# Half-step preparation of a squared-ReLU attention: one pair of v split eight steps earlier, and the first z block's scaling taken out of the opening

## The chip, the cores and the metric

The kernel runs on one core of a Trainium2 chip. The metric is the device time of one execution in microseconds (us). The kernel before took 1279.15 us (median of 3 runs, 1277.88 to 1280.24). Engines are named as the profile names them: PE multiplies matrices, PEld loads its weights, DVE and ACT are the two elementwise engines that matter here, SP issues the DMAs. Each engine works through its own list of instructions in order, and waits where an instruction needs something from another engine.

## The reference

Two stages stand behind each other. The first is an attention without softmax, in which keys and queries are the same array z, and the second is a soft mixture of experts on its output:

```
scores = (1/S) * z @ z.T                # per batch: 8 batches, S = 2496 tokens, 64 wide
attn   = max(scores, 0) ** 2
x      = u * (attn @ v)                 # v, u: 256 wide
logits = x @ phi                        # 32 slots; softmax over tokens and over slots
slot_input = softmax_tokens(logits).T @ x
slot_out   = relu(slot_input @ w1[e]) @ w2[e]      # 8 experts, 4 slots each
out        = softmax_slots(logits) @ slot_out
```

Inputs and outputs are 32-bit floats.

## The kernel before

**Tiles.** A batch's tokens stand in five blocks of 512 (j or p from 0 to 4). A chunk is one block of queries. A "half" is one chunk of queries against 256 keys, that is two key tiles of 128. A chunk has 10 halves, a batch 50 (the last batch 60), and `halves` is the list of all of them, with the number k counting through. The keys of v come in ten pairs of tiles per batch, `v_{batch}_{pair}`; a half uses one pair, or half of what such a pair covers in two neighbouring halves.

**One half** goes through `prepare(k)` (line 430) and `sums_halves` or `sums_whole` (line 541 and below). In `prepare`, PE multiplies z with z into a score tile `sc` (`scores`), ACT applies the ReLU and then the square (`r<-sc`, `r<-r` in the profile), ACT or DVE casts the result to 16 bits (`ph`, the high part), and DVE subtracts that from the 32-bit value (`pl`, the low part). PE then adds three products to `acc`: high v times `ph`, low v times `ph`, high v times `pl`. Because z times z is symmetric, a prepared half is also turned by DVE (`y<-r`), stored, and read back for the chunk that meets it the other way round; such a "turned" half needs no scores, only the cast and the subtraction.

**Order.** The main loop (line 1026) goes through the halves h. At step h it issues transfers, prepares half h+2 (h+3 from step 18 on) and multiplies half h. In `sums_halves` the twelve matmuls of phase 0 come first, then the scores of the half that is being prepared, then the twelve of phase 1. A list `behind` holds work that runs at the end of a `prepare`, and `landing[step]` puts work there. Every instruction of PE, ACT, DVE and SP stays in the order in which the program writes it (`InOrder`).

**v and z in two parts.** Each pair of v is loaded in 32 bits (`vr`), multiplied with a power of two per pair (`v_by`), and split into a high part by ACT (`v<-vr,v_by`) and a low part by DVE (`v<-vr,v_by,v`). The same is done with z. For batches 1 to 7 the table `v_at` (line 895) gives the step of the batch before, at which each of the ten pairs is split; numbers from 50 on lie in the batch itself.

**The opening.** Batch 0 has no batch before it. Its z blocks stay in `zraw`, slices of the tile `cw`. `measure_z` finds a power of two for each block (`z_by`), `raise_z(p)` (line 977) multiplies block p with it in place on DVE (`cw<-cw,z_by`), and the first 12 halves take their scores from these blocks in 32 bits. The first two halves go another way: `first_scores`, a square, and `plain_sums` in 32 bits with unscaled v, while v is still being measured. `scale_v` then finds v's common factor: one small matmul on PE (`idle<-ident,few`) and five small DVE operations. `keep_busy(n)` issues 2n matmuls of ones whose result nobody reads. After half 2 is prepared, the opening multiplies z blocks 2, 3 and 4 in a row, then prepares half 3, and the main loop begins.

All four engines are called through one helper, so nearly all rows of the profile carry line 74; rows are told apart by engine and tile name.

Of the kernel before, what the change touches and what calls it, by code (L numbers as in the profile page):

```python
# [8 lines left out]
F32 = mybir.dt.float32  # L9
# [5 lines left out]
ALU = mybir.AluOpType  # L15
# [3 lines left out]
P = 128  # L19
# [5 lines left out]
KT = 20  # L25
# [6 lines left out]
NP = KT // 4  # L32
# [45 lines left out]
def attn_soft_moe_kernel(ctx, tc, uT, v, zz, phi, ww, outT):  # L78
# [9 lines left out]
    cpool = ctx.enter_context(tc.tile_pool(name="cpool", bufs=1))  # L88
# [14 lines left out]
    zt, vt_, zraw, vraw = {}, {}, {}, {}  # L103

    nudge = cpool.tile([P, 1], F32, name="nudge")
    ones = nc.const_aps.tensor(1.0, [P, 512], BF16)

    def pair(name, n):
# [318 lines left out]
                start=(k == 0 and t == 0), stop=(k == 1 and t == 1),  # L427
            )

    def prepare(k, r=None):  # L430

        x = halves[k]
        n = x.ch[2]

        parts = [slice(0, 2)]
        if x.turned:
            whole = arriving.pop(k)
            run(middle)
        elif r is not None:
            run(middle)  # L440
            act.activation(r, r, AF.Square)
            whole = r.rearrange("p h (a r) -> p h a r", r=P)
        else:
            r = wa.tile([P, 2, QC], F32, tag="r", name=f"r_{k}", bufs=4)
            ps, m = scores(k)
            for h in parts:
                act.activation(r[:, h, :m], ps[:, h, :m], AF.Relu, scale=2.0**-22)
                run(middle)
                act.activation(r[:, h, :m], r[:, h, :m], AF.Square)
            whole = r[:, :, :m].rearrange("p h (a r) -> p h a r", r=P // 2 if x.borrows else P)  # L450
        hi, lo = high_low(k)
        m = QC if x.padded else n
        hc, lc = (t[:, :, :m].rearrange("p h (a r) -> p h a r", r=P) for t in (hi, lo))
        cast = act.copy if x.turned or (x.turns and x.at % 3 and k > 2) else dve.tensor_copy
        run(turning)
        pieces = [(whole, slice(0, P), cast)]
        if x.borrows:
            lent = arriving.pop(k)
            pieces = [(lent, slice(0, P // 2), act.copy), (whole, slice(P // 2, P), dve.tensor_copy)]
        for h in parts:  # L460
            for src, cols, cast in pieces:
                cast(hc[:, h, :, cols], src[:, h])
                dve.tensor_sub(lc[:, h, :, cols], src[:, h], hc[:, h, :, cols])
        pend[k] = hi, lo
        if x.turns:
            key = x.b, x.ch[0], x.p
            first = key not in staged
            if first:
                staged[key] = turns_sb.tile([P, 16, 4, NS], F32, tag="y", name=f"y_{k}")
            y = staged[key]  # L470

            def turn():
                dve.transpose(
                    y.rearrange("p m i q -> p i m q")[:, 2 * x.w : 2 * x.w + 2],
                    r.rearrange("p h (m q) -> p h m q", q=NS),
                )
                if not first:
                    stores.append((k + (k < 2 * NP), lambda: store(key)))

            if k < 2 * NP:  # L480
                turning.append(turn)
            else:
                turn()
        if x.lends:
            y = turns_sb.tile([P, 4, 2, 2, NS], F32, tag="yd", name=f"yd_{k}", bufs=1)
            dve.transpose(
                y.rearrange("p a j i q -> p i a j q"),
                r.rearrange("p h (a i q) -> p h a i q", i=4, q=NS)[:, :, :, 2:4],
            )
            stores.append((k - 1, lambda: lend(x, y)))  # L490
        run(behind)
# [49 lines left out]
    def sums_halves(k, acc, phase, before):  # L541


        x = halves[k]
        todo = [[], []]
        hi, lo = pend[k]
        for t, kt in enumerate(x.tiles):
            vt = vt_[x.b, kt // 2][:, kt % 2]
            hh, lh, hl = (vt[:, 0], hi[:, t]), (vt[:, 1], hi[:, t]), (vt[:, 0], lo[:, t])
            if kt < KT - 1:  # L550
                for h in range(2):
                    todo[h] += [hh, lh, hl]
            else:

                todo[0] += [hh] if phase else [hh, lh]
                todo[1] += [hl] if phase else [lh, hl]
        for i in range(len(todo[0])):
            for h, rows in enumerate(HALF):
                vp, pp = todo[h][i]
                c = h ^ phase ^ side[0]  # L560
                mm = pe.matmul(
                    totals(acc, c, x), vp[rows, c * P : (c + 1) * P], columns(pp[rows], x),
                    start=(x.starts and phase == 0 and i == 0),
                    stop=(x.ends and phase == 1 and i == len(todo[0]) - 1),
                )
                if before is not None:
                    await_(mm, before)
                    before = None
        if phase == 0:
            turn = nc.gpsimd.nop()  # L570
            await_(turn, mm)
            return turn
        side[0] ^= 1
# [317 lines left out]
    for b in range(1, B):  # L891
        base, order = (b - 1) * 2 * NP * NQ, BLOCKS[b == B - 1]
        z_at = [27, 28, 29, 30, 39 if b == B - 1 else 41]
        v_from = [23, 24, 25, 26, 27, 28, 29, 32, 33, 34]
        v_at = [41, 42, 43, 44, 45, 46, 48, 50, 52, 54]
        if b == B - 1:
            v_at = [42, 43, 44, 45, 46, 48, 52, 53, 41, 50]
        for i, (j, at) in enumerate(zip(order, z_at)):
            splits.setdefault(base + 9 + 2 * i, []).append((load_z, b, j, [base + 12 + 2 * i, base + at]))
        for i, (start, at) in enumerate(zip(v_from, v_at)):  # L900
            splits.setdefault(base + start, []).append(
                (load_v, b, i, [base + start + 1, base + at, base + at])
            )
        later[base + 23] = lambda b=b: add_bounds(b, next_acc(), slice(0, NP))
        later[base + 24] = lambda b=b: factors(b, accs[-1], slice(0, NP))
        later[base + 36] = lambda b=b: largest(b)
        later[base + 39] = lambda b=b: scale_v(b, ms_ps.tile([P, 2, 512], F32, tag="ms", name=f"mx_{b}"))
# [57 lines left out]
    def keep_busy(n):  # L965
        for _ in range(n):
            for h, rows in enumerate(HALF):
                pe.matmul(plain[:, h], ones[rows, 0:P], ones[rows], start=True, stop=True)
# [8 lines left out]
    def raise_z(p):  # L977
        dve.tensor_scalar_mul(zraw[0, p], zraw[0, p], z_by[0][:, p : p + 1])
# [9 lines left out]
        factors(0, idle, js)  # L988

    measure_z(slice(0, 1))  # L990
    raise_z(0)
    keep_busy(3)
    acc = next_acc()
    r0, relu = first_scores(0, scale=2.0**-30)
    relu()
    act.activation(r0, r0, AF.Square)
    r1, relu = first_scores(1, acc, scale=2.0**-30)
    relu()
    keep_busy(4)
    measure_z(slice(1, NP))  # L1000
    raise_z(1)
    dve.tensor_mul(r1, r1, r1)
    plain_sums(0, r0, plain, 0)
# [6 lines left out]
    first_v.pop()(dve)  # L1010
    largest(0)
    plain_sums(1, r1, plain, 0)
    scale_v(0, idle)
    plain_sums(1, r1, plain, 1)
    prepare(2, r2)
    split_first_v()
    split_first_v()
    for p in range(2, NP):
        raise_z(p)
    ratio = few[0][:, 3:4]  # L1020
    dve.tensor_scalar_mul(ratio, v_by[0][:, 0:1], 2.0**16)
    xg_[0] = wk.tile([P, 2, 1024], F32, tag="xg", name="xg_0")
# [3 lines left out]
    for h, x in enumerate(halves):  # L1026
        if x.begins and h:
            chunk = h // (2 * NP)
            acc = accs[chunk] if chunk < len(accs) else next_acc()
        last = len(halves) - h  # L1030
        transfers(h)
        if x.b < NW_OWN and h % (2 * NP * NQ) == 2 * NP * (NQ - 1) + 5:
            load_w(x.b)
        if h < 2:
            continue
        weights(last)
        if work and (x.at > 1 or last <= 20):
            work.pop(0)()
        behind.extend(landing.pop(h, ()))
        ahead = [k for k in range(h + 2 + (h > CATCH), h + 3 + (h >= CATCH)) if k < len(halves)]  # L1040
        split_first_v()
        if ahead and not halves[ahead[0]].turned:
            turn = sums_halves(h, acc, 0, None)
            prepare(ahead.pop(0))
            sums_halves(h, acc, 1, turn)
        else:
            if ahead and not x.ends:
                prepare(ahead.pop(0))
            elif not ahead:
                run(middle)  # L1050
                run(behind)
                between_last(3 - last)
            sums_whole(h, acc)
        if x.ends:
            finish_chunk(x.b, x.ch, acc)
        for k in ahead:
            prepare(k)
        if h in FIRST_Z:
            z_splits.pop(FIRST_Z[h])()
        del pend[h]  # L1060
# [303 lines left out]
```

## Time and profile before

| | us |
|---|---|
| median of 3 runs | 1279.15 |
| the profiled execution's own time | 1278.43 |
| its span, first to last instruction | 1276.6 |
| PE busy in the span | 1247.4 (98%) |
| DVE busy | 1099.7 (86%) |
| ACT busy | 930.2 (73%) |
| PE waiting for DVE's `pl`, whole span | 3.3 in 5 waits |
| PE waiting for DVE's `v`, whole span | 2.3 in 7 waits |
| PE waiting for ACT's `ot`, in the last stage | 11.2 in 14 waits |

The busy time of PE counts each matmul's own duration, and two matmuls on the two halves of PE's rows run side by side, so the pace of PE is read from the starts of its rows rather than from its busy share. A row of the timeline gives the start, the duration, the engine, the operation, "out<-in", how many instructions are merged in the row, and in brackets how long the engine sat idle before it and for whom.

### The profile page before, as it was taken

What the parts mean: (1) busy time and instruction counts of PE and PEld (TensorE: products, weight loads), DVE (VectorE), ACT (ScalarE), POOL (GpSimd) and SP (SyncE); (2) the same over time, 40 slices, a digit from 0 to 9 for tenths busy, and PEclk for the clock granted to TensorE, in tenths of its full rate; (3) what the DMA queues carried; (4) which work ended last, traced back from release to release, by engine and by line L of the source; (5) the groups of instructions that cost most, each with busy time, mean ns of one, the idle gap of its engine ahead of it and who ended that gap; (6) DMA issues with size and microseconds to landing.
All of it is one profiled execution on the core that took longest, in us unless ns stands there. A gap on an engine that the chain in (4) does not pass through costs nothing.

```text
span 1276.6 us, 27277 instructions
## 1 busy us (share of the span) xinstructions
PE 1247.4 (98%) x10931; PEld 634.7 (50%) x10931; DVE 1099.7 (86%) x1594; ACT 930.2 (73%) x1209; POOL 3.7 (0%) x22
## 2 busy tenths in 40 slices
PE   9999999999999999999999999999999999999984
PEld 4445454545445444555445454454545445445752
DVE  7888899789998899889998899898998899886663
ACT  6878797687958788586977778587885879664553
POOL 0000000000000000000000000000000000000000
PEclk9999999999999999999999999999999999999985
DMA  5769668794879757795779757987488766889769
GB/s 167 222 185 300 219 151 252 223 295 129 219 256 299 226 154 203 244 315 189 185 219 293 238 170 180 288 281 262 122 238 246 287 184 159 262 245 337 276 260 383
DMA packets 132942, 298.83 MB, mean 234 GB/s; under 512 B 14416, under 2 KB 35408, under 8 KB 120784
## 3 DMA queue, kind: packets, MB, share of 16 engines
q1 hardware_dynamic: 132816, 297.10, 75.1%
q8 instruction: 85, 1.39, 0.4%
q14 instruction: 41, 0.34, 0.1%
HBM read 162.04 MB, written 113.77 MB: 216 GB/s over the span
## 4 chain that ended last, share of the span: by engine, by line
PE 88%; DVE 6%; ACT 2%; issue 2%; DMA 1%; DVEq 0%; ACTq 0%; SPq 0%
PE acc L74 71%; PE sc L74 10%; PE lg L74 2%; DVE y L74 2%; PE pf L74 2%; DVE pl L74 2%; ACT r L74 1%; PE plain L74 1%; DVE v L74 1%; ACT ot L74 1%; PE po L74 1%; PE h L74 1%; DVE ph L74 1%; DMA outT<-ot 0%; ACT ph L74 0%
## 5 line engine op out<-in xcount | busy, mean ns | idle before, releaser
L74 PE MATMUL acc<-ph,v 64*128 64x512 f16 (+4 forms) x5004 | 935.9, 368 | 2.4 <-DVE v L74 2.3
L74 PEld LDWEIGHTS <-v 64*128 64x128 f16 (+1 forms) x7506 | 490.6, 95 | 500.4 <-issue 39.6
L74 PE MATMUL acc<-pl,v 64*128 64x512 f16 (+5 forms) x2502 | 621.8, 368 | 3.4 <-DVE pl L74 3.3
L74 DVE TENSOR_TENSOR pl<-r,ph 128x1024 f16<-128x1024 f32 (+1 forms) x408 | 464.9, 1146 | 103.8 <-ACT ph L74 79.9
L74 ACT CAST ph<-r 128x1024 f16<-128x1024 f32 (+1 forms) x285 | 288.4, 1019 | 129.0 <-DMA r<-turned 69.5
L74 ACT ACTIVATE r<-sc 128x1024 f32<-128x1024 f32 (+1 forms) x241 | 228.1, 947 | 115.5 <-PE sc L74 109.8
L74 ACT ACTIVATE r<-r 128x1024 f32<-128x1024 f32 (+1 forms) x241 | 237.8, 987 | 6.8
L74 DVE STREAM_TRANSPOSE y<-r 128x1024 f32<-128x1024 f32 x160 | 198.1, 1238 | 0.0
L74 PE MATMUL sc<-z,z 64*128 64x512 f16 x912 | 128.2, 376 | 0.4 <-ACT r L74 0.2
L74 PEld LDWEIGHTS <-z 64*128 64x128 f16 x1380 | 75.6, 94 | 70.5 <-issue 2.7
L74 DVE CAST ph<-r 128x1024 f16<-128x1024 f32 (+1 forms) x123 | 73.5, 598 | 11.1 <-ACT r L74 10.6
L74 ACT ACTIVATE v<-vr,v_by 128x512 f16<-128x512 f32 x80 | 57.4, 719 | 10.4 <-DVE v_by L74 9.6
L74 DVE SCALAR_TENSOR_TENSOR xg<-acc,out_by,ut 128x1024 f32<-128x1024 f32 (+7 forms) x56 | 50.2, 921 | 12.3 <-PE acc L74 12.3
L74 DVE SCALAR_TENSOR_TENSOR v<-vr,v_by,v 128x512 f16<-128x512 f32 x80 | 58.5, 733 | 0.0
L74 PE MATMUL sc<-z 64*128 64x512 f16 (+1 forms) x468 | 52.9, 321 | 0.0
L74 DVE STREAM_TRANSPOSE y<-xg 128x512 f32<-128x512 f32 x72 | 49.5, 688 | 0.0
L74 ACT ACTIVATE vq<-vr 128x512 bf16<-128x512 f32 x75 | 46.7, 623 | 3.7 <-DMA vr<-in_v 3.6
L74 DVE COPY ot<-pf 128x1024 f32<-128x1024 f32 (+1 forms) x20 | 24.0, 1198 | 18.1 <-PE pf L74 18.1
L74 ACT COPY ot<-pf 128x1024 f32<-128x1024 f32 (+1 forms) x20 | 19.8, 992 | 22.8 <-PE pf L74 21.2
L74 DVE SCALAR_TENSOR_TENSOR z<-zr,z_by,z 128x512 f16<-128x512 f32 x35 | 25.7, 735 | 0.0
L74 DVE STREAM_TRANSPOSE yd<-r 128x512 f32<-128x512 f32 x36 | 25.4, 704 | 0.0
L74 ACT ACTIVATE z<-zr,z_by 128x512 f16<-128x512 f32 x35 | 25.1, 718 | 0.0
(196 smaller groups left out, 545.3 us busy)
## 6 DMA issues: line engine op xcount, KB each, us to landing
turned<-y SPq DMA_DIRECT2D x320, 256.0 KB, 5.0
r<-turned SPq DMA_DIRECT2D x76, 1024.0 KB, 8.1
xt<-y SPq DMA_DIRECT2D x72, 288.0 KB, 5.6
vr<-in_v SPq DMA_DIRECT2D x80, 256.0 KB, 5.9
outT<-ot SPq DMA_DIRECT2D x18, 1024.0 KB, 7.0
ut<-in_uT SPq DMA_DIRECT2D x31, 512.0 KB, 5.9
lent<-yd SPq DMA_DIRECT2D x144, 64.0 KB, 3.1
rd<-lent SPq DMA_DIRECT2D x36, 256.0 KB, 3.6
```

Of the source, the lines that this page charges most:

```text
L74: return lambda *a, **k: self.tc.keep_in_program_order(f(*a, **k))
```

## The change

Three things are edited. First, in batches 1 to 6 the last pair of v (pair 9) is split at step 46 of the batch before instead of at step 54 (its own batch's fifth step), and pair 0 at step 40 instead of 41. Second, the first two halves take their scores from the z block as it was loaded; its factor goes into the ReLU's scale, as a column `lift` that holds the square of the factor times 2^-30. `raise_z(0)` then runs behind all measurements, the `keep_busy` groups of three and four become one of five, and the raising of blocks 2, 3 and 4 moves from the opening into the main loop, to steps 2, 4 and 6, each directly in front of the step's `prepare`. Third, half 2's cast to 16 bits moves in front of `scale_v`, its subtraction stays behind it, and half 2's matmuls are reordered: both tiles' `ph` with high v first, then both `pl`, then both `ph` with low v.

```diff
+    lift = cpool.tile([P, 1], F32, name="lift")
...
-    def prepare(k, r=None):
+    def prepare(k, r=None, between=None):
...
         for h in parts:
             for src, cols, cast in pieces:
                 cast(hc[:, h, :, cols], src[:, h])
+                if between is not None:
+                    between()
                 dve.tensor_sub(lc[:, h, :, cols], src[:, h], hc[:, h, :, cols])
...
             hh, lh, hl = (vt[:, 0], hi[:, t]), (vt[:, 1], hi[:, t]), (vt[:, 0], lo[:, t])
-            if kt < KT - 1:
+            if k == 2:
+                for h in range(2):
+                    todo[h][t:t] = [hh]
+                    todo[h][2 * t + 1 : 2 * t + 1] = [hl]
+                    todo[h].append(lh)
+            elif kt < KT - 1:
                 for h in range(2):
                     todo[h] += [hh, lh, hl]
...
-        v_at = [41, 42, 43, 44, 45, 46, 48, 50, 52, 54]
+        v_at = [40, 42, 43, 44, 45, 46, 48, 50, 52, 46]
...
     measure_z(slice(0, 1))
-    raise_z(0)
-    keep_busy(3)
+    dve.tensor_scalar(lift, z_by[0][:, 0:1], z_by[0][:, 0:1], 2.0**-30, op0=ALU.mult, op1=ALU.mult)
     acc = next_acc()
-    r0, relu = first_scores(0, scale=2.0**-30)
+    r0, relu = first_scores(0, scale=lift)
     relu()
     act.activation(r0, r0, AF.Square)
-    r1, relu = first_scores(1, acc, scale=2.0**-30)
+    r1, relu = first_scores(1, acc, scale=lift)
     relu()
-    keep_busy(4)
+    keep_busy(5)
     measure_z(slice(1, NP))
+    raise_z(0)
     raise_z(1)
     dve.tensor_mul(r1, r1, r1)
...
-    scale_v(0, idle)
-    plain_sums(1, r1, plain, 1)
-    prepare(2, r2)
+
+    def factor():
+        scale_v(0, idle)
+        plain_sums(1, r1, plain, 1)
+
+    prepare(2, r2, factor)
     split_first_v()
     split_first_v()
-    for p in range(2, NP):
-        raise_z(p)
...
         transfers(h)
+        if h in (2, 4, 6):
+            raise_z(1 + h // 2)
```

The order of instructions at three places shows what moved. In these rows `v_0_4` is pair 4 of batch 0, `pl_3` the low part of half 3, `sc_6` the scores of half 6, `cw_78` a z block of batch 0; the number at a name's end only tells tiles apart. The brackets name the engines' semaphores that a row waits for.

DVE, from the end of the opening to the first main-loop steps, before:

```order
L74 TENSOR_TENSOR pl_2_295<-r_2_253,ph_2_294 128x1024 [waits DVE_49]
L74 SCALAR_TENSOR_TENSOR v_0_2_133<-vr_0_2_151,v_by0_88,v_0_2_133 128x2x256 [waits DMAHW7_49,Activation_49]
L74 SCALAR_TENSOR_TENSOR v_0_3_134<-vr_0_3_153,v_by0_88,v_0_3_134 128x2x256 [waits DMAHW0_49,Activation_49]
L74 TENSOR_SCALAR cw_78<-cw_78,z_by0_84 128x512 x3
L74 TENSOR_SCALAR few0_92<-v_by0_88 128x1
L74 STREAM_TRANSPOSE y_2_298<-r_2_253 128x2x16x32
L74 CAST ph_3_314<-r_3_308 128x1024 [waits Activation_49]
L74 TENSOR_TENSOR pl_3_315<-r_3_308,ph_3_314 128x1024 [waits DVE_49]
L74 SCALAR_TENSOR_TENSOR v_0_4_135<-vr_0_4_155,v_by0_88,v_0_4_135 128x2x256 [waits Activation_49]
```

and with the change:

```order
L74 TENSOR_TENSOR pl_2_285<-r_2_251,ph_2_284 128x1024
L74 SCALAR_TENSOR_TENSOR v_0_2_134<-vr_0_2_152,v_by0_89,v_0_2_134 128x2x256 [waits DMAHW7_49,Activation_49]
L74 SCALAR_TENSOR_TENSOR v_0_3_135<-vr_0_3_154,v_by0_89,v_0_3_135 128x2x256 [waits DMAHW0_49,Activation_49]
L74 TENSOR_SCALAR few0_93<-v_by0_89 128x1
L74 STREAM_TRANSPOSE y_2_296<-r_2_251 128x2x16x32
L74 CAST ph_3_309<-r_3_303 128x1024 [waits Activation_49]
L74 TENSOR_TENSOR pl_3_310<-r_3_303,ph_3_309 128x1024 [waits DVE_49]
L74 TENSOR_SCALAR cw_78<-cw_78,z_by0_85 128x512
L74 SCALAR_TENSOR_TENSOR v_0_4_136<-vr_0_4_156,v_by0_89,v_0_4_136 128x2x256 [waits Activation_49]
```

The three multiplications stood in front of half 3's transpose, cast and subtraction; now one of them, that of block 2, stands behind `pl_3`. Blocks 3 and 4 stand in the same way directly behind `pl_5` and `pl_7`.

PE, around the scores of half 6 (the first half whose keys lie in block 3), before:

```order
L74 LDWEIGHTS v_0_4_135
L74 MATMUL acc_0_217<-pl_4_343,v_0_4_135 128x512
L74 MATMUL sc_6_419<-cw_78 128x512 [waits Activation_49]
L74 MATMUL sc_6_419<-cw_78 128x512
L74 LDWEIGHTS v_0_4_135 [waits Pool_sequencer_49]
```

and with the change:

```order
L74 LDWEIGHTS v_0_4_136
L74 MATMUL acc_0_212<-pl_4_339,v_0_4_136 128x512
L74 MATMUL sc_6_416<-cw_78 128x512 [waits DVE_49,Activation_49]
L74 MATMUL sc_6_416<-cw_78 128x512
L74 LDWEIGHTS v_0_4_136 [waits Pool_sequencer_49]
```

The scores of half 6 now wait for DVE too, where they waited for ACT alone. The scores of half 8 gained the same wait; those of half 4 waited for DVE before as well, for a multiplication that stood further ahead.

DVE, at the end of step 46 of a batch (here batch 0, whose successor's pairs are `v_1_...`), before:

```order
L74 TENSOR_TENSOR pl_49_1951<-r_49_1940,ph_49_1950 128x8x64 [waits DVE_49]
L74 STREAM_TRANSPOSE y_1_1891<-xg_1_1439 128x4x4x32
L74 SCALAR_TENSOR_TENSOR v_1_5_536<-vr_1_5_1304,v_by1_89,v_1_5_536 128x2x256 [waits Activation_49]
L74 CAST ph_50_1994<-r_50_1984 128x1024 [waits PE_49,Activation_49]
L74 TENSOR_TENSOR pl_50_1995<-r_50_1984,ph_50_1994 128x1024 [waits DVE_49,PE_49]
```

and with the change:

```order
L74 TENSOR_TENSOR pl_49_1949<-r_49_1938,ph_49_1948 128x8x64 [waits DVE_49]
L74 STREAM_TRANSPOSE y_1_1889<-xg_1_1437 128x4x4x32
L74 SCALAR_TENSOR_TENSOR v_1_5_534<-vr_1_5_1302,v_by1_90,v_1_5_534 128x2x256 [waits Activation_49]
L74 SCALAR_TENSOR_TENSOR v_1_9_539<-vr_1_9_1491,v_by1_90,v_1_9_539 128x2x256 [waits DMAHW0_49,PE_49,Activation_49]
L74 CAST ph_50_1994<-r_50_1984 128x1024 [waits PE_49,Activation_49]
L74 TENSOR_TENSOR pl_50_1995<-r_50_1984,ph_50_1994 128x1024 [waits DVE_49,PE_49]
```

The low part of pair 9 stands behind that of pair 5. Before, it stood between half 57's transpose and half 58's subtraction.

## The prediction, made before the changed kernel was run

> **What bounds the kernel now.** I read first for what PE waits (waits, by engine), then the chain of work that ended last, then the timeline at the places that the change touches.
>
> ```profile
> PE acc L74 <- DVE pl L74: 3.3, 5, 0.7
> PE acc L74 <- DVE v L74: 2.3, 7, 0.7
> ```
>
> PE waits little by this count (total us, times, longest), and these two waits are the ones that the change can reach. The chain tells more:
>
> ```profile
> 27.50 2.59 PE acc L74 x24
> 30.09 0.86 PE sc L74 x4
> ...
> 42.93 0.75 DVE v L74
> ...
> 52.43 1.24 DVE pl L74
> ```
>
> A step of PE is 24 matmuls in 2.59 us, 12 pairs side by side at 0.216, plus 0.86 for a half's 32-bit scores: 3.45 us. But from 42.93 to 53.67 the chain runs through DVE, one operation behind the other, and PE is not on it. So in the first dozen steps ACT and DVE set the pace, and PE has no half in reserve. Later it has, but for one place in each batch (last part of the sum).
>
> **The change part by part.** Each term is worked out as times in the profiled execution. First the opening, up to the scores of half 4:
>
> ```profile
> 5.77 0.15 DVE L74 TENSOR_SCALAR z_by<-z_by 128x1 f32<-128x1 f32 x1
> 5.95 0.49 DVE L74 TENSOR_SCALAR cw<-cw,z_by 128x512 f32<-128x512 f32 x1
> 6.36 0.68 DVE L74 CUSTOM_DVE_ANT_0 sq<-cw 128x512 bf16<-128x512 f32 x1
> 10.56 0.49 DVE L74 TENSOR_SCALAR cw<-cw,z_by 128x512 f32<-128x512 f32 x1
> 10.96 1.22 DVE L74 TENSOR_TENSOR r<-r 128x1024 f32<-128x1024 f32 x1
> 17.05 0.29 DVE L74 TENSOR_REDUCE few<-idle 128x2 f32<-128x128 f32 x1 [0.64 <-PE idle L74]
> 18.03 0.69 DVE L74 CAST ph<-r 128x1024 f16<-128x1024 f32 x1
> 18.75 1.23 DVE L74 TENSOR_TENSOR pl<-r,ph 128x1024 f16<-128x1024 f32 x1
> 19.62 0.38 PE L74 MATMUL acc<-ph,v 64*128 64x512 f16 x2
> 19.89 1.41 DVE L74 SCALAR_TENSOR_TENSOR v<-vr,v_by,v 128x512 f16<-128x512 f32 x2
> 20.70 0.39 PE L74 MATMUL acc<-ph,v 64*128 64x512 f16 x2 [0.69 <-DVE v L74]
> 20.89 1.06 ACT L74 ACTIVATE r<-r 128x1024 f32<-128x1024 f32 x1
> 21.22 1.28 DVE L74 TENSOR_SCALAR cw<-cw,z_by 128x512 f32<-128x512 f32 x3
> 21.85 1.13 PE L74 MATMUL sc<-cw 64*128 64x512 f32 x4
> 22.47 1.24 DVE L74 STREAM_TRANSPOSE y<-r 128x1024 f32<-128x1024 f32 x1
> 23.63 0.66 DVE L74 CAST ph<-r 128x1024 f16<-128x1024 f32 x1
> 24.32 1.23 DVE L74 TENSOR_TENSOR pl<-r,ph 128x1024 f16<-128x1024 f32 x1
> ```
>
> The `lift` operation works on one column; like the `z_by` row it needs about 0.17 (0.18 from start to start), in the place of a multiplication that held DVE 0.41 (5.95 to 6.36): 0.24 gained. The same multiplication comes back in front of block 1's (0.40, 10.56 to 10.96): 0.16 lost, and v's measuring, which follows on DVE without a pause, is 0.16 later. That the first scores start over a microsecond earlier, and that PE does four filler matmuls fewer, changes nothing: DVE's chain decides when v's factor is there.
>
> Half 2's cast (0.72, 18.03 to 18.75) moves into DVE's idle 0.64 in front of 17.05; it overhangs by 0.08. So v's factor comes 0.24 later, and the subtraction `pl_2` starts at 18.03 + 0.24 = 18.27, not 18.75. PE starts half 2 at 19.62 + 0.16 = 19.78, finds `pl_2` and the low v in time, loses the wait of 0.69, and ends phase 0 (1.29) at 21.07. The row in front of its scores of half 4 says 21.85, so by itself this gains 0.78.
>
> But the scores of half 4 now need a multiplication that stands behind `pl_3` on DVE. From `pl_2`: low v at 18.27 + 1.14 = 19.41 (18.75 to 19.89 before), the pair of them 1.33 (19.89 to 21.22), a small operation of less than 0.1, the transpose 1.16 from start to start, so half 3's cast could start at 21.97; its square on ACT ends at 21.95 + 0.16, so it starts at 22.17. Then 0.69 to `pl_3`, 1.14 to the multiplication (24.00), 0.49 and 0.06 until PE sees it: **24.55 instead of 21.85, 2.7 us late**, with PE standing still for 3.5 us. Queued behind these scores on PE are phase 1 of half 2 and all that follows; behind them on ACT, the ReLU of half 4.
>
> The same happens twice more, and there the loop closes over ACT:
>
> ```profile
> 22.78 0.63 PE L74 MATMUL acc<-ph,v 64*128 64x512 f16 x4
> 23.01 1.03 ACT L74 ACTIVATE r<-sc 128x1024 f32<-128x1024 f32 x1 [0.45 <-PE sc L74]
> 25.16 1.05 ACT L74 CAST ph<-r 128x1024 f16<-128x1024 f32 x1
> 29.68 1.05 ACT L74 CAST ph<-r 128x1024 f16<-128x1024 f32 x1
> 29.91 1.04 PE L74 MATMUL sc<-cw 64*128 64x512 f32 x4
> 31.26 1.00 ACT L74 ACTIVATE r<-sc 128x1024 f32<-128x1024 f32 x1
> 34.87 1.01 ACT L74 ACTIVATE r<-sc 128x1024 f32<-128x1024 f32 x1
> 36.80 1.04 PE L74 MATMUL sc<-cw 64*128 64x512 f32 x4
> 41.78 1.23 DVE L74 TENSOR_TENSOR pl<-r,ph 128x1024 f16<-128x1024 f32 x1 [0.66 <-ACT ph L74]
> ```
>
> Scores of half 4 to its ReLU: 1.16 (21.85 to 23.01). ReLU to cast: 2.15 (23.01 to 25.16). Cast to the ReLU of half 5: 1.58 (29.68 to 31.26), as ACT splits a pair of v in between. Its cast again 2.15 later, 1.05 long; then 0.06, `pl_5` 1.14, the multiplication 0.49 and 0.06. From scores 4 to scores 6 that is 1.16 + 2.15 + 1.58 + 2.15 + 1.05 + 0.06 + 1.14 + 0.55 = 9.84 us, where PE's own work in between is 0.93 (21.85 to 22.78) + 2.59 + 3.45 = 6.97. So scores 6 come at 34.39, not 29.91. From scores 6 to scores 8 ACT has no cast but the copy `xg` between the two ReLUs, 3.61 in all (31.26 to 34.87): 1.16 + 3.61 + 2.15 + 1.05 + 0.06 + 1.14 + 0.55 = 9.72, so **scores 8 come at 44.11 instead of 36.80, 7.3 us late**.
>
> Some of it comes back, since ACT has nothing queued up then: `pl_8` started 4.98 after its scores (36.80 to 41.78) and now 1.16 + 2.15 + 1.05 + 0.06 = 4.42: 0.56 regained. From `pl_8` on DVE's list is the one of before, and by the chain it ran there without a pause until `pl_11` ended at 53.67. So **6.7 us** stay. This term could be between 0, if the three multiplications end before PE comes to them, and 7.3.
>
> The third part, in batches 1 to 6:
>
> ```profile
> 190.32 0.71 DVE L74 SCALAR_TENSOR_TENSOR v<-vr,v_by,v 128x512 f16<-128x512 f32 x1
> 190.43 0.40 PE L74 MATMUL acc<-ph,v 64*128 64x512 f16 x2
> 191.09 0.39 PE L74 MATMUL acc<-ph,v 64*128 64x512 f16 x2 [0.27 <-DVE v L74]
> ```
>
> This is pair 9's low part, and PE reaching it: 0.66 between two pairs instead of 0.216, so 0.44 is lost. Of the seven waits for `v`, the 0.69 of the opening is one; the other six are 1.6 us together, 0.27 each, one per batch 1 to 6. Split at step 46 this part is there long before: 6 x 0.44 = **2.6 us gained**. What the move adds at step 46 is one operation of about 0.7 on ACT and on DVE, and both have room a few microseconds on:
>
> ```profile
> 164.61 1.02 ACT L74 ACTIVATE r<-sc 128x1024 f32<-128x1024 f32 x1 [0.80 <-PE sc L74]
> 167.83 1.22 DVE L74 TENSOR_TENSOR pl<-r,ph 128x1024 f16<-128x1024 f32 x1 [0.76 <-ACT ph L74]
> ```
>
> ACT stands still 0.80 and DVE 0.76 there, and PE's five waits for `pl` all lie in the first 81 us. Were that cover gone, PE would wait up to 0.7 six times, 4.3 lost; pair 0's one step earlier hides in the same place. I take 2.6 gained, with nothing gained as the near bound.
>
> **Sum**: 6.7 - 2.6 = 4.1. The profiled execution took 1278.43, so 1282.5; the median lies 0.7 above it, so **1283.2 us**.
>
> **Rivals.** (a) *The clock*. PE's first matmuls run at half pace:
>
> ```profile
> 0.77 3.60 PE L74 MATMUL plain<-const-bfloat16-1.0 64*128 64x512 bf16 x16 [0.77 <-PEq L1354]
> ```
>
> 8 pairs in 3.60 are 0.45 each against 0.216. If standing still for 3.5 us puts PE back to that pace, scores 4 take 0.9 longer and everything behind them shifts by that; after the other two stalls (9.84 - 6.97 = 2.9, and 2.8) the same at most: 0.9 to 2.7 more, 1284.1 to 1285.9. Nothing in the trace shows PE idle so long, for or against. The Trainium skill ("TensorE: Matmul & The Clock Gate", section "Part 1: The HAM clock gate") has the clock halved after an idle window of about 3.4 us that runs freely; by that rule the first stall may just do it and the others not, and the sum would be 1284.1.
>
> (b) *The lag is made up.* PE's waits for `pl` behind 30 us are 2.6 of the 3.3. Were DVE's work done ahead during the stalls, these would vanish: 6.7 - 2.6 - 2.6 = 1.5, so 1280.6, no measurable change. Against it: DVE's operations there depend on ACT's results, and those on the late scores.
>
> (c) *Faster*: the multiplications are done before PE needs them. That decides at 21.07, where PE ends phase 0: if block 2 is multiplied by then, scores 4 come 0.78 earlier and `pl_3` at 22.86 instead of 24.32, so PE gains up to 1.5 in the opening and 2.6 later: 1275.1. For it speaks that 1.28 us of DVE work leave the path to `pl_3`; against it, that DVE's own list puts `pl_3` first.
>
> (d) *Pair 9's move gains nothing*, because the next operation in DVE's list is late in its place: 1285.8. Against it: the next row that PE reads there is a subtraction that it did not wait for.
>
> **Chances**: the forecast 0.58, (a) 0.15, (b) 0.14, (c) 0.06, (d) 0.07. A measurement of this kernel can tell about 0.2% from no change, here 2.6 us, so slower begins at 1281.7: the forecast, (a) and (d) make 0.80. Within 0.2%: (b), 0.14. Faster: (c), 0.06. The forecast's own range is 1282 to 1284.5; with part of (b) at one end and (a) and (d) at the other it is 1280.5 to 1286.
>
> **What would show it.** In the changed kernel's waits a new line, PE's `sc` waiting for DVE's `cw`, three times, about 9 us in all, between 21 and 45 us; scores 4, 6 and 8 about 9.8 us apart; PE's waits for `v` at the batches' beginnings gone. If scores 6 start at about 30 us, the step over DVE's order is wrong; if PE's pairs behind 24.5 us stand 0.43 apart, (a) holds; if `pl_11`'s readers come under 5 us late, the part on what comes back is wrong.

## The result, and the profile after

The changed kernel took 1287.4 us (median of 5 runs, 1285.84 to 1291.26) against 1278.5 of the kernel before in the same comparison: ratio 1.007, 95% interval 1.0059 to 1.0081, so 7.5 to 10.4 us slower, 8.9 by the medians. A sixth run, of 4605.92 us, was in the slow state and is left out here; with it the median is 1288.6. The forecast was 1283.2, 4.1 slower, with 1286.0 as the upper end: the sign was right, the size less than half of what was measured.

The profiled execution took 1287.44 us, span 1285.7, which is 9.1 us more than before. PE's waits, in its view by engine (total us, times, longest):

```profile
PE sc L74 <- DVE cw L74: 8.3, 3, 3.4
PE acc L74 <- DVE pl L74: 3.2, 6, 0.7
PE acc L74 <- ACT ph L74: 1.1, 1, 1.1
```

The new line for the multiplied z is there, three times, 8.3 us; the waits for `v` are gone; and there is a wait for `ph` that nobody had forecast. The timeline of the changed kernel at the three stalls:

```profile
22.40 1.23 DVE L74 TENSOR_TENSOR pl<-r,ph 128x1024 f16<-128x1024 f32 x1
23.54 0.48 DVE L74 TENSOR_SCALAR cw<-cw,z_by 128x512 f32<-128x512 f32 x1
24.17 1.19 PE L74 MATMUL sc<-cw 64*128 64x512 f32 x4 [3.39 <-DVE cw L74]
25.10 1.11 PE L74 MATMUL acc<-ph,v 64*128 64x512 f16 x4
25.93 1.13 PE L74 MATMUL acc<-pl,v 64*128 64x512 f16 x4
...
35.46 2.08 PE L74 MATMUL sc<-cw 64*128 64x512 f32 x4 [2.44 <-DVE cw L74]
37.58 1.02 ACT L74 ACTIVATE r<-sc 128x1024 f32<-128x1024 f32 x1 [3.29 <-PE sc L74]
...
46.68 1.13 PE L74 MATMUL sc<-cw 64*128 64x512 f32 x4 [2.44 <-DVE cw L74]
```

`pl_3`, the multiplication, the scores: the order is the one forecast, at 24.17 instead of 24.55. But scores 4, 6 and 8 stand 11.29 and 11.22 apart, not 9.84 and 9.72. Two rows show why. Behind 25.10 two pairs of PE take 0.83 (25.10 to 25.93), 0.42 each instead of 0.216; and the scores of half 6 take 2.08 us instead of 1.13, so their ReLU starts 2.12 behind them instead of 1.16. PE ran at half clock. The trace's record of the granted clock changes at 25.11, 28.53, 35.35 and 38.77; cut at these instants, the windows (start and end, then busy us and instructions of PE, PEld, DVE, ACT and POOL, the granted clock, the DMA share and GB/s) read:

```profile
21.70:25.11 3.41, 0.94 (x5) 0.47 (x7) 3.38 (x5) 0.55 (x1) 0.00 (x0) 1.00 0.00 0
25.11:28.53 3.42, 3.42 (x19) 1.77 (x17) 0.73 (x1) 3.07 (x4) 0.00 (x0) 0.50 0.54 117
31.94:35.35 3.41, 1.08 (x11) 0.39 (x6) 1.66 (x3) 2.31 (x3) 0.00 (x0) 1.00 0.59 223
35.35:38.77 3.42, 3.31 (x12) 1.45 (x14) 1.78 (x2) 1.16 (x2) 0.00 (x0) 0.50 0.42 134
42.18:45.59 3.41, 2.06 (x20) 0.84 (x16) 1.99 (x3) 3.26 (x4) 0.00 (x0) 1.00 0.38 100
45.59:49.01 3.42, 2.33 (x18) 1.34 (x20) 2.76 (x4) 1.13 (x2) 0.00 (x0) 1.00 0.02 5
```

Two windows in which PE was busy for 0.94 and 1.08 of 3.41 us are each followed by one at 0.50. The third stall falls across two windows, PE is busy for over 2 us in both, and the clock stays.

Laid beside the trace of before, matmul by matmul, the shift is +9.88 at the scores of half 8, +9.28 once half 8 is through, and then falls by 0.44 or 0.45 at each of six batch beginnings (2.65 in all), where the 0.66 between two pairs is now 0.22 (200.13 to 200.35):

```profile
199.70 0.61 PE L74 MATMUL acc<-ph,v 64*128 64x512 f16 x4
200.13 0.40 PE L74 MATMUL acc<-pl,v 64*128 64x512 f16 x2
200.35 0.59 PE L74 MATMUL acc<-ph,v 64*128 64x512 f16 x3
```

It rises twice: by 0.55 at half 172 and by 2.02 at half 272, both the 23rd half of a batch, a turned half that is fetched by DMA. ACT, which casts it, waits for the transfer, and PE for ACT (at half 172 for the subtraction on DVE that follows the cast). At half 272:

```profile
835.17 1.99 ACT L74 CAST ph<-r 128x1024 f16<-128x1024 f32 x2 [10.36 <-DMA r<-turned]
836.26 0.61 PE L74 MATMUL acc<-ph,v 64*128 64x512 f16 x4 [1.14 <-ACT ph L74]
```

In the trace of before PE waited at neither place. Its rows at half 172, ACT's cast, DVE's two subtractions and the first matmul that reads one of them, were:

```profile
529.53 1.99 ACT L74 CAST ph<-r 128x1024 f16<-128x1024 f32 x2 [8.46 <-DMA r<-turned]
530.61 2.36 DVE L74 TENSOR_TENSOR pl<-r,ph 128x1024 f16<-128x1024 f32 x2 [4.93 <-ACT ph L74]
...
532.24 0.38 PE L74 MATMUL acc<-pl,v 64*128 64x512 f16 x2
```

The first of the two subtractions takes 1.22 us, so it ended 0.41 before PE came to it; at half 272 the same margin was 0.63.

So 9.28 - 2.65 + 2.57 = 9.2 (9.1 by the spans). Three things had to be told apart: whether the stalls alone make the forecast 6.7, what the half clock costs, and why two fetches that were in time before are late now.

### The profile page after: what moved, and what is told of

Its sections match the earlier page's. It is cut to its first block, busy times and chain, and to the rows that moved or that the text cites. A ratio compares the mean times of both kernels' runs of the same rounds, so it can differ in the third digit from the quotient of the medians.

```text
span 1285.7 us, 27266 instructions
## 1 busy us (share of the span) xinstructions
PE 1249.0 (97%) x10927; PEld 643.3 (50%) x10927; DVE 1099.2 (85%) x1595; ACT 929.1 (72%) x1209; POOL 3.7 (0%) x22
## 4 chain that ended last, share of the span: by engine, by line
PE 87%; DMA 4%; DVE 3%; ACT 3%; SPq 1%; issue 1%; ACTq 0%; DVEq 0%
PE acc L74 70%; PE sc L74 11%; PE lg L74 2%; DMA turned<-y 2%; PE pf L74 2%; DMA r<-turned 1%; ACT r L74 1%; SPq L74 1%; DVE pl L74 1%; ACT ot L74 1%; PE po L74 1%; PE h L74 1%; DVE y L74 1%; DMA outT<-ot 0%; ACT ph L74 0%
## 5 line engine op out<-in xcount | busy, mean ns | idle before, releaser
L74 PEld LDWEIGHTS <-v 64*128 64x128 f16 (+1 forms) x7506 | 497.7, 95 | 493.7 <-issue 43.9
```

Source lines behind the costliest of these rows:

```text
L74: return lambda *a, **k: self.tc.keep_in_program_order(f(*a, **k))
```

## The experiments

Each is timed against the kernel before on its own chip, but not all on one chip; a ratio r is turned into us as (r - 1) x 1279.

**Pair 9 alone.**

```diff
-        v_at = [41, 42, 43, 44, 45, 46, 48, 50, 52, 54]
+        v_at = [40, 42, 43, 44, 45, 46, 48, 50, 52, 46]
```

> The kernel before with the move of v's pairs 9 and 0 alone. Theory (stalls in the opening, a gain of 0.44 at each of six batch beginnings): 2.65 us faster than before, about 1275.9 us; PE's waits for v fall from 7 to 1; the start of every half in batch 0 is unmoved. Rival (the move gains nothing, or what it brings is lost at halves 172 and 272, where the changed kernel waited for fetched halves): 1278 to 1278.5 us, with PE waiting for ph at half 22 of a batch.

1276.36 us against 1279.18, ratio 0.9982 (0.9973 to 0.9992): 2.3 gained (1.0 to 3.5). PE's view by engine has one wait for `v` left, that of the opening:

```profile
PE acc L74 <- DVE pl L74: 3.2, 5, 0.7
...
PE acc L74 <- DVE v L74: 0.7, 1, 0.7
```

The shift falls by 0.44 to 0.46 at the same six places, 2.7 together, and before the last stage nowhere else changes by 0.25 or more: no loss at halves 172 and 272. This term was right.

**The opening alone**, the changed kernel with that table taken back.

> The changed kernel with v's pairs 9 and 0 back at their old steps: the changes of the opening alone. Theory: about 9.3 us slower than before, 1287.8 us; PE waits three times for the multiplied z, over 8 us in all, and pairs stand 0.43 apart for 3.4 us behind the first two of these waits. Rival (the losses of 0.55 and 2.02 at halves 172 and 272 come from batch 0 being late, not from the move): 1290 us or more, with the same two waits for ph.

1292.96 us, ratio 1.0107 (1.0094 to 1.0120): 13.7 slower. That is more than the theory had (9.3) and fits the rival (1290 us or more): the two waits for `ph` are there without the move of pair 9, so that move does not make them. The timeline of its scores 4, 5, 6, 7 and 8:

```profile
24.31 1.13 PE L74 MATMUL sc<-cw 64*128 64x512 f32 x4 [3.39 <-DVE cw L74]
27.84 1.05 PE L74 MATMUL sc<-cw 64*128 64x512 f32 x4
34.17 1.13 PE L74 MATMUL sc<-cw 64*128 64x512 f32 x4 [2.69 <-DVE cw L74]
37.69 1.05 PE L74 MATMUL sc<-cw 64*128 64x512 f32 x4
43.93 1.13 PE L74 MATMUL sc<-cw 64*128 64x512 f32 x4 [2.60 <-DVE cw L74]
```

In this execution the clock stayed at 1.00 in the opening, although the code and the stalls are those of the changed kernel. Scores 4, 6 and 8 are 9.86 and 9.76 apart and the shift settles at 6.53. The forecast of the stalls (9.84, 9.72, 6.7) holds as soon as the clock does. The rest is at the two fetches: the shift grows by 4.74 at half 172 and by 4.16 at half 272, half clock behind both included. Its windows there:

```profile
538.25:541.66 3.41, 0.71 (x12) 0.30 (x5) 1.02 (x1) 2.09 (x3) 0.00 (x0) 1.00 0.95 304
541.66:545.08 3.42, 3.16 (x16) 1.36 (x17) 3.32 (x6) 1.88 (x2) 0.00 (x0) 0.50 0.41 158
...
838.62:842.03 3.41, 1.17 (x18) 0.55 (x12) 1.75 (x2) 2.82 (x3) 0.00 (x0) 1.00 0.87 265
842.03:845.45 3.42, 3.42 (x20) 1.46 (x18) 3.32 (x6) 2.23 (x4) 0.00 (x0) 0.50 0.54 205
```

**The multiplications back in front of half 3**, the rest as changed; and **each multiplication one half earlier** than in the change.

```diff
     split_first_v()
     split_first_v()
+    raise_z(2)
...
-        if h in (2, 4, 6):
-            raise_z(1 + h // 2)
+        if h in (3, 5):
+            raise_z((h + 3) // 2)
```

That is the second one; the first has the old loop over blocks 2 to 4 there, and none in the main loop.

> The changed kernel with the multiplications of blocks 2 to 4 back in front of half 3, everything else as changed. Theory (the three late multiplications make the whole loss): no wait of the scores for the multiplied z over 0.5 us, no half clock behind 6 us, scores of half 4 at about 21.2 us; 0.3 to 0.8 gained in the opening and 2.65 later, so 1275.0 to 1275.6 us. Rival (the unmultiplied first scores or the cast in front of v's factor cost something too): 1278 us or more, with the start of half 2 or of half 4 later than before.

> The changed kernel with each late multiplication one half earlier in VectorE's order: block 2 in front of half 3, block 3 in front of half 5's work, block 4 in front of half 7's, each two halves ahead of the scores that read it. Theory (the place in VectorE's order makes the stall, not that the block is multiplied late): scores of half 4 at about 21.2 us, no stall at 4, 6 or 8, no half clock; as fast as with all three in the opening or up to 0.8 faster, 1274.5 to 1275.6 us. Rival (any multiplication in the loop delays the chain over ACT and DVE): up to 0.5 us lost at each of two places, 1276 to 1277 us.

1276.91 us, ratio 0.9983 (0.9975 to 0.9992), and 1276.83 us, 0.9983 (0.9974 to 0.9991). Neither has a wait for the multiplied z among its waits or half a clock before the last stage. Scores 4 with the multiplications in front of half 3, then scores 4, 6 and 8 with each one half earlier:

```profile
20.93 1.13 PE L74 MATMUL sc<-cw 64*128 64x512 f32 x4
```

```profile
20.68 1.13 PE L74 MATMUL sc<-cw 64*128 64x512 f32 x4
...
27.94 1.04 PE L74 MATMUL sc<-cw 64*128 64x512 f32 x4
...
34.84 1.04 PE L74 MATMUL sc<-cw 64*128 64x512 f32 x4
```

So the place in DVE's order makes the stalls, and a multiplication in the main loop is free where it stands one half earlier: the opening gains 0.96 and 1.85 in the two traces. Both lose 2.5 (1.79 + 0.68, 0.95 + 1.49) at halves 172 and 272 again. So the second one's 1276.83 lies where its rival had it, but not for the rival's reason: nothing is lost at the multiplications, and without the loss at the two fetches both would have come near 1275.

**The moved addresses.** The four executions with the new opening so far had late fetches, the two with the old one had not. One thing that the diff does shows in no engine's list: `lift` is a tile of its own, and every SBUF buffer that is allocated behind it moves by 32 bytes. The next runs take `lift` into a spare column of an existing tile, or move the addresses of the kernel before.

```diff
-    lift = cpool.tile([P, 1], F32, name="lift")
...
+    lift = few[1][:, 3:4]
```

> The run with each multiplication one half earlier, but the factor `lift` now in a spare column of an existing tile, so that every buffer keeps the SBUF address that it has in the kernel before (with a tile of its own for `lift`, all that is allocated after it moves by 32 bytes). Theory (the moved addresses change how long the DMA packets take, and make the fetches for halves 172 and 272 late): no wait for ph there, the DMA queue's share back at 75% from 73%, and the median 1.3 to 2.4 us lower than with the moved addresses, 1274.4 to 1275.5 us. Rival (the new opening, or chance, makes those fetches late): unchanged at 1276.8 us, with waits for ph.

> The changed kernel with `lift` in a spare column: the change without the moved addresses. Theory: 6.5 us (no half clock) to 9.3 us (two intervals of it) lost in the opening and 2.65 gained later, so 1283.0 to 1285.8 us, and no wait for ph at halves 172 and 272. Rival (opening or chance makes the fetches late): 1287 to 1291 us as the changed kernel.

```diff
+    spare = cpool.tile([P, 1], F32, name="spare")
+    dve.memset(spare, 0.0)
```

> The kernel before with one unused tile of one column in `lift`'s place and one small memset of it, so that all addresses behind it move by 32 bytes; nothing else. Theory (addresses): 1.3 to 2.4 us slower than before, 1280.5 to 1281.6 us, PE waiting for ph at half 22 of batch 3 or 5, the DMA queue's share about 73%. Rival (opening or chance): 1279.2 us as before, no such wait.

The kernel before with nothing but that unused column took 1282.83 us, ratio 1.0031 (1.0017 to 1.0046): **4.0 us slower** (2.2 to 5.9), more than the 1.3 to 2.4 expected, its twelve runs spread from 1278.4 to 1289.0. In its trace PE waits for ACT at the same two halves:

```profile
532.61 1.99 ACT L74 CAST ph<-r 128x1024 f16<-128x1024 f32 x2 [9.39 <-DMA r<-turned]
533.71 0.61 PE L74 MATMUL acc<-ph,v 64*128 64x512 f16 x4 [0.38 <-ACT ph L74]
...
830.08 1.99 ACT L74 CAST ph<-r 128x1024 f16<-128x1024 f32 x2 [9.66 <-DMA r<-turned]
831.18 0.61 PE L74 MATMUL acc<-ph,v 64*128 64x512 f16 x4 [0.67 <-ACT ph L74]
```

The shift against before grows by 1.26 and 1.56 there. (It starts 1.5 late in this execution, because PE's full clock came at 10.0 us instead of 5.97; that instant lies between 3.5 and 10.0 in the traces, whatever the kernel.) The change without the moved addresses took 1285.39 us, 1.0052 (1.0040 to 1.0064), 2.3 less than the change by the two ratios, which come from different comparisons and whose intervals overlap. The variant with each multiplication one half earlier took 1275.54 us, ratio 0.9971 (0.9960 to 0.9981), where it had 0.9983 (0.9974 to 0.9991); these intervals overlap too.

The waits that were expected to go did not all go. With the addresses kept, the trace of this variant still lost 1.97 at half 272, with PE waiting 1.1 for `ph`, and the trace of the change 0.83 there, with PE waiting 0.65 for the `pl` behind the late cast. The two further runs below that have the new opening and the addresses kept lost at these places too, 0.64 with the filler and 0.53 + 0.77 with one late multiplication. Among the executions without moved addresses only the two with the old opening, before and pair 9 alone, were free of it. So the lateness of these fetches does not come from the addresses alone; it goes with the new opening too, and by what path is not shown.

**Which addresses, and how far.** Three more edits of the kernel before: the same buffers moved by 64 bytes (a spare tile of 16 columns); a spare column in front of the pool of the turned halves only; and one behind the buffers of z and v.

> The kernel before with an unused tile of 16 columns and a small memset, so that the same addresses move by 64 bytes instead of 32. Theory (what counts is where a buffer lies within 64 bytes: 32 into them before, 0 after a move by 32): as before, 1279 us, queue's share 75%. Rival (any move of the addresses costs, or the additional tile and memset do): about 1282.8 us, as with 32 bytes, share 73%.

> The kernel before with an unused tile of one column in a pool of its own right in front of the pool of the turned halves, so that these buffers alone (stored, and fetched again) move by 32 bytes. If they carry the whole effect: 1282 to 1283 us, queue's share about 73%, waits for ph at half 22 of batch 3 or 5. If it comes from the other buffers (loads of v and z, the shifted xt): 1279 us, share about 75%.

> The kernel before with an unused tile of one column behind the buffers into which z and v are loaded, so that everything allocated after them (the shifted xt, E, y, the turned halves) moves by 32 bytes and the buffers of z and v, raw and split, stay. If the effect of 32 bytes comes from what lies behind (the transfers y to xt just ahead of the late fetch): about 1282 us. If it comes from the buffers of z and v: 1279 us.

| moved | by | ratio, interval | us | DMA queue's share in its profile |
|---|---|---|---|---|
| all behind `lift`'s place | 32 | 1.0031, 1.0017 to 1.0046 | +4.0 | 73.3% |
| all behind `lift`'s place | 64 | 1.0006, 0.9997 to 1.0015 | +0.8 | 73.7% |
| turned halves only | 32 | 1.0001, 0.9992 to 1.0010 | +0.1 | 73.5% |
| all behind the buffers of z and v | 32 | 1.0026, 1.0015 to 1.0037 | +3.3 | 73.3% |

A move by 64 does not cost what a move by 32 does, so the additional tile and memset are not the cost. The buffers of z and v have no part that can be seen, and the turned halves alone do not carry it. What is left is what lies between (the tiles of the second stage, `xt`, `E`, `y` and `xg` among them, and its weights), alone or together with the turned halves. One rival stays: the move by 64 and that of the turned halves were timed on one chip, the two moves by 32 that cost time on two others, so a difference between chips is not excluded. The share of the queue, 75.1% before, fell in all four and tells nothing of the time: there the expectation was wrong. The profiled executions of the three kernels that moved 64 bytes, the turned halves only, or all behind z and v also lost 1.2 to 1.9 us at halves 172 and 272, so one execution alone does not separate them; the medians do.

**Filler in the stalls.** The change without moved addresses, and in front of scores 4, 6 and 8 matmuls of ones that nobody reads:

```diff
+            if k in (4, 6, 8):
+                for _ in range(12 if k == 4 else 9):
+                    for h, rows in enumerate(HALF):
+                        pe.matmul(idle[:, h], ones[rows, 0:P], ones[rows], start=True, stop=True)
             ps, m = scores(k)
```

> The run before this one (the change without the moved addresses) plus filler: 12 pairs of unneeded matmuls in front of the scores of half 4 and 9 pairs in front of those of halves 6 and 8, at 0.216 us a pair 2.6 and 1.95 us, inside PE's stalls of 3.4 and 2.4 us. Theory (PE's idle time makes the half clock, which costs the rest): clock 1.0 throughout the opening, scores 4, 6 and 8 about 10 us apart, 6.5 us lost in the opening, so 1283.0 us, at or below the run without filler by 0 to 2.8 us, as that had no or two intervals of half clock. Rival (the spacing of 11.3 us comes from ACT and DVE, not from the clock): no gain, and up to 0.3 us lost to the fillers' ends.

1284.03 us, ratio 1.0040 (1.0028 to 1.0052), against 1285.39 without. The timeline of scores 4, 6 and 8, and the window of the whole opening:

```profile
25.52 1.13 PE L74 MATMUL sc<-cw 64*128 64x512 f32 x4 [0.77 <-DVE cw L74]
...
35.38 1.13 PE L74 MATMUL sc<-cw 64*128 64x512 f32 x4 [0.72 <-DVE cw L74]
...
45.16 1.13 PE L74 MATMUL sc<-cw 64*128 64x512 f32 x4 [0.64 <-DVE cw L74]
```

```profile
18.00:60.00 42.00, 39.58 (x298) 20.22 (x297) 32.72 (x43) 31.78 (x37) 0.00 (x0) 1.00 0.53 128
```

9.86 and 9.78 apart, clock 1.00, and from the start of half 2 to behind half 8 it loses 6.71 against before (1.05 to 7.76). Without filler the trace of the same kernel had half clock behind the first and the third stall and lost 9.26 (-0.37 to 8.89):

```profile
31.33:34.74 3.41, 1.63 (x16) 0.70 (x12) 1.92 (x2) 2.82 (x4) 0.00 (x0) 1.00 0.41 126
34.74:38.16 3.42, 2.77 (x22) 1.60 (x24) 2.33 (x4) 1.57 (x2) 0.00 (x0) 1.00 0.53 209
41.57:44.98 3.41, 0.99 (x10) 0.32 (x6) 2.49 (x4) 2.39 (x3) 0.00 (x0) 1.00 0.60 150
44.98:48.39 3.41, 3.22 (x12) 1.36 (x14) 1.85 (x3) 1.08 (x2) 0.00 (x0) 0.50 0.24 50
```

The emptiest window of the opening with filler, 23.09 to 26.51, has PE busy for 2.65 of 3.42 us. So the mechanism is shown in the traces: more work for PE, 2.5 us less. In the medians it is 1.4 less with intervals that overlap, so what the clock costs on average lies between nothing and some 3 us.

**One late multiplication**, block 4 alone.

> The change without moved addresses, with blocks 2 and 3 multiplied in front of half 3 and only block 4 late, behind half 7's work: one stall instead of three. Theory: scores 8 come 9.72 us behind scores 6 (about 29.0), so at 38.7 us, PE stands for about 2.5 us, of which 0.56 comes back at half 8; against 1275.5 us without a stall that is 1.9 to 2.5 us more, 1277.4 to 1278.0 us, and 1.5 us on top where the window of the clock takes the stall in whole. Rival (the stalls do not add up, one alone is hidden by later slack): 1275.5 us.

1279.34 us, ratio 0.9998 (0.9989 to 1.0007). Timeline and windows at its one stall:

```profile
39.40 2.08 PE L74 MATMUL sc<-cw 64*128 64x512 f32 x4 [2.86 <-DVE cw L74]
```

```profile
36.01:39.43 3.42, 0.56 (x8) 0.10 (x4) 2.80 (x4) 2.18 (x3) 0.00 (x0) 1.00 0.97 335
39.43:42.84 3.41, 3.41 (x12) 1.51 (x14) 1.64 (x2) 1.29 (x2) 0.00 (x0) 0.50 0.94 315
```

Scores 8 came 9.93 behind scores 6 (29.47), and the shift grew by 3.66, of which the half clock is about 1.5, an estimate from the 1.43 and 1.46 of the changed kernel. By the ratios, which come from two chips, it is 3.4 above the variant without a stall (0.9971). So one stall alone is not hidden by later slack, and it carries its own risk of half a clock.

## Why the prediction was right in sign and wrong in size

- **The stalls: right.** "6.7 us stay" is 6.6 when it is counted from the start of half 2, which the forecast had 0.16 later. Counted so, it was measured as 6.69 and 6.71 in the two traces whose clock stayed (6.53 + 0.16, and 7.76 - 1.05), and the steps behind it as 9.86 and 9.76, 9.86 and 9.78. The loop over ReLU, cast, `pl`, multiplication and scores was read from rows of before that had nothing to do with each other yet, and it held to 0.1. The regained 0.56 came as 0.60.
- **Start of half 2: not borne out.** The forecast was 0.16 later; it started 0.31 earlier. Between executions of the same old opening this start lies anywhere from 19.07 to 21.13, with the instant at which PE's clock becomes full, so a term of 0.16 could neither be won nor lost in a single trace.
- **Pair 9's move: right.** 2.65 in the trace, 2.3 in the medians, forecast 2.6; rival (d) falls. Rival (b) falls too: PE's waits for `pl` are still 3.2 us.
- **The clock: the step that failed first.** It stood as rival (a) at 0.15 and with nothing in the sum, and its likeliest price was one interval, 0.9. The profiled execution had two, at 1.43 and 1.46 each (11.29 - 9.86, 11.22 - 9.76): besides PE's own matmuls, the scores themselves run at half pace, and everything behind them on ACT and DVE waits. "Nothing in the trace shows PE idle so long" was no reason to leave it out of the sum; half pace at the start was in the trace, and the stalls were forecast at 2.8 to 3.5. The trace of before even had the sign that no such pause is needed: in its last stage a window of 3.41 us in which PE was busy for 1.60 (1224.53 to 1227.94), and waited 0.93 and 0.88 at the longest, is followed by one at 0.50.
- The Trainium skill ("TensorE: Matmul & The Clock Gate", section "Part 1: The HAM clock gate") has the clock halved after an idle window of about 3.4 us that runs freely. The traces agree on the length (3.41 in every window above) and on the free run, for the same opening had two, two others or no halved windows in three executions. They differ on idle: 12 to 34% busy was enough.
- **An effect that no step had: the two fetches, and the addresses.** The sum had nothing for them, and the profiled execution lost 2.57 there. `lift` was costed as an operation of 0.17 on DVE and as nothing else. As a tile it moved the buffers of the second stage by 32 bytes, and that by itself costs 4.0 us in the kernel before; in the changed one the same kind of difference is 2.3, with intervals that overlap. Part of the lateness stays when the new opening keeps the addresses, so they are not the only cause, and how much of the 2.57 is theirs is open. The fetches had little to spare (0.41 and 0.63 us in the trace of before), and no wait showed that, since nobody waited.

The terms add up: 4.1 forecast, 2.9 for the two intervals of half clock and 2.6 at the fetches, less 0.5 for the start of half 2 (0.31 earlier instead of 0.16 later), make the 9.1 of the trace.

With the two left out the sum is borne out: without moved addresses and at full clock (the run with filler) the change costs 5.1 us (3.6 to 6.7) where 4.1 was forecast. Rival (c), the multiplications done before PE asks for them, gave 1275.1; the version that does this, with each one a half earlier and no moved address, took 1275.54 and has the lowest ratio of all, 0.29% below the kernel before (0.19 to 0.40).

## What to carry to other kernels

An operation is not free because its result is wanted late: look at what stands ahead of it in its engine's list, and move it by one item rather than next to its reader. When a forecast makes PE stand for two to four microseconds, put the half-clock interval behind it into the sum, here at about 1.5 us times the chance that a window takes the stall. A transfer that lands just in time shows in no wait, so look at its margin before you move what stands ahead of it. A new tile is an edit of every address behind it: put small values into spare columns, or run the old kernel with the same tile added before anything else is blamed.

## What the runs showed of the hardware

Half clock follows a window of 3.41 us in which PE was busy too little, not a pause of a given length:

| window (us) | kernel | PE busy | next window |
|---|---|---|---|
| 21.09 to 24.50 | change, addresses kept | 12% | half |
| 36.01 to 39.43 | one late multiplication | 16% | half |
| 538.25 to 541.66 | opening alone | 21% | half |
| 21.70 to 25.11 | change | 28% | half |
| 41.57 to 44.98 | change, addresses kept | 29% | half |
| 31.94 to 35.35 | change | 32% | half |
| 838.62 to 842.03 | opening alone | 34% | half |
| 39.91 to 43.32 | opening alone | 42% | full |
| 19.43 to 22.84 | opening alone | 44% | full |
| 31.33 to 34.74 | change, addresses kept | 48% | full |

The limit lies between 34 and 42% in these stages; in the last stage, with other matmuls, half clock also followed windows that the same count has at 47 to 58%, so the share is not the whole rule. Pauses of 2.44 us did it or did not, by where the window cut them.

Moving SBUF buffers by 32 bytes, with every instruction the same but one small memset, cost 0.31%, and 0.26% on a second chip where those of z and v stayed; moving them by 64, on a third chip, cost nothing that can be measured (below 0.15%). Through which transfer this works, and why the DMA queue's share fell in all four kernels whose addresses moved while only two became slower, stays open.
